# Gated linear attention and an MLP on one core: x of chunks 2 to 5 turned by DMA instead of TensorE

## The chip, the core and the metric

The kernel runs on one NeuronCore of a Trainium2 chip. Its engines work side by side, each through its own instructions in the order of the program: TensorE (PE) multiplies matrices and writes to PSUM; VectorE (DVE), ScalarE (ACT) and GpSimd (POOL) work element by element; SyncE (SP) only issues DMAs. They wait for each other by semaphores. The metric is the device time of one execution in microseconds (us), lower is better.

## The reference

Per batch (4) and head (8), a state of 48 x 48 runs over 768 tokens; its output, the eight heads side by side, is the input x of a block with layer norm, two matrix products and a residual:

```
state = alpha[t][:, None] * state + outer(k[t], v[t]);  y[t] = q[t] @ state
x  = y of all heads, 384 columns
xn = (x - mean(x)) / sqrt(var(x) + 1e-6) * g_ln
out = x + maximum(xn @ w_ch1, 0) @ w_ch2          # 384 -> 1536 -> 384
```

Everything is float32.

## The kernel before, in words

The 768 tokens are cut into six chunks of 128. One chunk of one batch, 128 tokens of all eight heads, is called a block here; there are 24. `attention(c, b)` is the work of a block, written as a generator: each `yield` ends a turn. In its first turn it takes the logarithm of alpha (`la`, L293), then come the running sums (L525, in `sums`), exponentials (L303, L304), the products with q and k (L312), the turning of q and k on TensorE (L349, copied from PSUM by L359), the scores (L541, masked by L383), the updates of the state (L399, L412, L414) and y (L440). ACT copies y to SBUF as `x` (L452 or L456), SP keeps a copy in DRAM (`kept`, L466), and ACT normalizes it to `xn` (L473 to L483).

The MLP wants x with columns on partitions, as `xT`. For chunks 2 to 5 (`c >= IN_HALVES`, 16 blocks) a float32 is seen as two 16-bit halves, and TensorE turns each half exactly, as bfloat16, in pieces of 64 x 64: 24 transposes a block (L506) into two PSUM banks. In the next turn ACT copies each bank to `xT`, putting the halves of a number together again (L510). Chunks 0 and 1 are turned in float32 (L490).

From chunk 1 on, the MLP's two products are made from 15 and 20 block products instead of the 18 and 24 that plain multiplication by blocks takes. So `combine_x` (L830) adds and subtracts blocks of `xT` on DVE, `hidden_product` (L856) multiplies, DVE and POOL add up (L866 to L899), ACT takes the Relu (L907), `combine_hidden` (L663) adds blocks of that, and `product` (L676) multiplies again and adds to the output (L686 to L755), which `send` (L555) stores. `outputs` (L551) loads the kept x again as `ob` for that.

The order of all this is written by hand. `ORDER` is a string of 1501 letters; each letter gives one generator one more turn: `a` to `x` are the 24 blocks, `M`, `V`, `N`, `X` and `R` the MLP, `O` the outputs, `0` to `3` the loads. Every engine gets its instructions in that order, and so does SP's one queue of DMAs.

Tiles with the same tag share buffers: `la`, `x` and `xn` share the tag "row" with eight buffers of 1.5 KB a partition, and all PSUM tiles share eight banks. A new tile takes the buffer that has been free longest, and its first writer waits until the last reader of the tile before has ended; if none is free by the program, the instruction waits for the first that becomes so.

Of the kernel before, what the change touches and what calls it, by code (L numbers as in the profile page):

```python
# [9 lines left out]
FP32 = mybir.dt.float32  # L10
# [3 lines left out]
BF16 = mybir.dt.bfloat16  # L14
UINT16 = mybir.dt.uint16
# [4 lines left out]
IN_HALVES = 2  # L20
# [31 lines left out]
def kernel(  # L52
# [36 lines left out]
    nc = tc.nc  # L89
# [4 lines left out]
    P = 128  # L94
# [3 lines left out]
    NF = DM // P  # L98
# [7 lines left out]
    work = ctx.enter_context(tc.tile_pool(name="work", bufs=2))  # L106
    dram = ctx.enter_context(
        tc.tile_pool(name="dram", bufs=B, space=bass.MemoryType.DRAM))
    ps = ctx.enter_context(tc.tile_pool(name="ps", bufs=2, space=bass.MemoryType.PSUM))
# [3 lines left out]
    HS = P // 2  # L113
    halves = [slice(HS * s, HS * s + HS) for s in range(2)]
# [60 lines left out]
    ident_of_halves = consts[:, 2 * P + HS:].bitcast(BF16)  # L175
# [96 lines left out]
    def qk_of(c, b):  # L272
        return qks[b if c == 0 else b ^ 1 if c == 1 else (b ^ 1) % 3]
# [6 lines left out]
    x_of, xT_of, hT_of, las, lps_of, qkT_of, aps_of, ob_of = ({} for _ in range(8))  # L280
# [3 lines left out]
    def attention(c, b):  # L284
# [26 lines left out]
        for n in (0, 1) if whole else (1, 0):  # L311
            nc.vector.tensor_mul(qk[:, n], raws.pop(("qk"[n], c, b)), (eq, lv)[n])  # L312
            if n == 0:
                row = dram.tile([2, 2 * 64 * NP], FP32, name="row", tag="row")
# [9 lines left out]
        if c < IN_HALVES:  # L324
            for i in range(2):
# [5 lines left out]
                tv = tps.rearrange("r p (s t) -> r p s t", s=2)  # L331
# [6 lines left out]
        else:  # L338
            words = qk_of(c, b).rearrange("t n p i c -> t (n p i c)").bitcast(BF16).rearrange(
                "t (n p i c w) -> t n p i c w", n=2, p=NP, i=2, w=2)  # L340
            tps = [ps.tile([P, 512], FP32, name=f"tps{h}", tag="bank", bufs=8) for h in range(2)]
            for n in range(2):
                for p in range(NP):
                    for w in range(2):
                        for i, cs in enumerate((slice(0, 64), slice(64, R))):
                            for h in range(2):
                                tv = tps[h].bitcast(BF16).rearrange(
                                    "r (n p w t) -> r n p w t", n=2, p=NP, w=2)
# [33 lines left out]
        else:  # L382
            nc.vector.copy_predicated(  # L383
                out=at.rearrange("k p s t -> k (p s) t"),
# [36 lines left out]
        for p in range(NP):  # L421
# [4 lines left out]
            for n in range(0 if whole else 8):  # L426

                if odd:
                    inner, s, i = n // 4, n // 2 % 2, n % 2
                    r = i  # L430
                else:
                    i, s, r = n // 4, n // 2 % 2, n % 2
# [17 lines left out]
        if odd:  # L450
            for r in range(2):
                act(out=x[:, r * DM // 2:][:, :DM // 2], func=AFT.Copy, accum_out=few[:, 4 + r:5 + r],  # L452
                    in_=yps[r][:, r].rearrange("t b d -> t (b d)"))
# [14 lines left out]
        xn = work.tile([P, DM], FP32, name="xn", tag="row", bufs=8)  # L468
# [9 lines left out]
        if whole:  # L478
            nc.vector.tensor_scalar(out=xn, in0=x, scalar1=mean, scalar2=rstd,
                                    op0=AOP.add, op1=AOP.mult)  # L480
        else:
            nc.scalar.mul(off, mean, rstd)
            act(out=xn, in_=x, func=AFT.Identity, scale=rstd, bias=off)  # L483
        yield
        if c not in xT_of:
            xT_of[c] = work.tile([P, NF, B, P], FP32, name="xT", tag="xT")
        if c < IN_HALVES:
            xps = ps.tile([P, NF, P], FP32, name="xps", tag="bank", bufs=8)
            for f in range(NF):
                nc.tensor.transpose(xps[:, f], xn[:, f * P:(f + 1) * P], ident)  # L490
            yield
            if whole:
                nc.vector.tensor_mul(xT_of[c][:, :, b], xps,
                                     g_col.unsqueeze(2).broadcast_to([P, NF, P]))
            else:
                nc.vector.tensor_copy(out=xT_of[c][:, :, b], in_=xps)
        else:
            words = xn.bitcast(BF16).rearrange("t (f i c w) -> t f i c w", f=NF, i=2, w=2)
            xps = [ps.tile([P, 512], FP32, name=f"xps{h}", tag="bank", bufs=8) for h in range(2)]
            for f in range(NF):  # L500
                for w in range(2):
                    for i in range(2):
                        for h in range(2):
                            tv = xps[h].bitcast(BF16)[:, :2 * NF * HS].rearrange(
                                "r (f w t) -> r f w t", f=NF, w=2)
                            nc.tensor.transpose(tv[halves[i], f, w], words[halves[h], f, i, :, w],  # L506
                                                ident_of_halves[halves[h]])
            yield
            for h in range(2):
                nc.scalar.copy(  # L510
                    out=xT_of[c][:, :, b, halves[h]].bitcast(UINT16).rearrange(
                        "r f (t w) -> r f t w", w=2),
                    in_=xps[h].bitcast(UINT16)[:, :2 * NF * HS].rearrange(
                        "r (f w t) -> r f t w", f=NF, w=2))
        yield


# [415 lines left out]
    turns |= {"PQ"[h]: second_of_chunk_0(h) for h in range(2)}  # L933
    turns |= {"4": sums(), "5": scores()}
    turns |= {chr(ord("a") + n): attention(n // B, n % B) for n in range(NCB * B)}
    turns |= {chr(ord("A") + i): take_weights(i) for i in range(len(pieces))}
    turns |= {"M": mlp(), "V": hidden_products(NCB - 1), "S": combine_first(), "W": combine_weights(), "R": relus(),
# [34 lines left out]
```

## Time and profile before

| | |
|---|---|
| three runs | 423.15, 423.38, 423.86 us; median 423.38 |
| profiled execution | 423.5 us, the span from its first to its last instruction |
| TensorE clock granted | 1.000 in the whole span |
| L506, turning x on PE | 384 instructions, one 186 to 217 ns, several at a time |
| L510, copying it from PSUM on ACT | 32 instructions, 491 ns each |
| L483, xn of the 20 blocks of chunks 1 to 5 on ACT | 707 ns each |
| DMAs issued by SP | 235, nearly 44 MB in all |

A busy time is the time in which an engine has at least one instruction under way; those of PE overlap, so a share near 100% says that PE is seldom without work, not that it is at its peak. The chain that ended last follows back, from the last instruction, what each step waited for. In lists by group, the numbers behind the bar are the busy time and the mean of one instruction in ns, then the idle time of the engine before them and who ended it.

### The profile page before, as it was taken

What the parts mean: (1) busy time and instruction counts of PE and PEld (TensorE: products, weight loads), DVE (VectorE), ACT (ScalarE), POOL (GpSimd) and SP (SyncE); (2) the same over time, 40 slices, a digit from 0 to 9 for tenths busy, and PEclk for the clock granted to TensorE, in tenths of its full rate; (3) what the DMA queues carried; (4) which work ended last, traced back from release to release, by engine and by line L of the source; (5) the groups of instructions that cost most, each with busy time, mean ns of one, the idle gap of its engine ahead of it and who ended that gap; (6) DMA issues with size and microseconds to landing.
All of it is one profiled execution on the core that took longest, in us unless ns stands there. A gap on an engine that the chain in (4) does not pass through costs nothing.

```text
span 423.5 us, 14142 instructions
## 1 busy us (share of the span) xinstructions
PE 416.0 (98%) x5988; PEld 366.6 (87%) x5988; DVE 326.9 (77%) x626; ACT 228.0 (54%) x572; POOL 155.2 (37%) x182
## 2 busy tenths in 40 slices
PE   7989999999999999999999999999999999999996
PEld 5878878756778889998889998899998899988996
DVE  3689989898998989778668667749676588756684
ACT  6987577969535879434666066496432541124300
POOL 4242010200116391244671334670145650656414
PEclk9999999999999999999999999999999999999999
DMA  7879866774533341161503136002122000130001
GB/s 234 242 210 276 259 180 187 229 224 146 115 109 122 97 147 45 38 180 30 150 23 111 61 90 159 0 22 39 42 82 70 0 2 0 39 112 2 0 20 56
DMA packets 50791, 43.95 MB, mean 104 GB/s; under 512 B 23164, under 2 KB 46844, under 8 KB 50728
## 3 DMA queue, kind: packets, MB, share of 16 engines
q1 hardware_dynamic: 50696, 43.04, 35.3%
q8 instruction: 47, 0.77, 0.8%
q14 instruction: 16, 0.13, 0.1%
q0 software_dynamic: 32, 0.00, 0.0%
HBM read 34.29 MB, written 8.74 MB: 102 GB/s over the span
## 4 chain that ended last, share of the span: by engine, by line
PE 91%; DVE 3%; DMA 3%; ACT 1%; issue 1%; SPq 1%; DVEq 0%
PE ops L676 31%; PE hps L856 31%; PE ops L576 7%; PE hps L564 7%; PE yps L440 5%; PE aps L541 2%; PE ups L399 2%; PE tps L349 2%; DMA ws<-in_moe_w_ch_dram 2%; PE lps L525 1%; DMA ra<-in_alpha_dram 1%; DVE qk L312 1%; PE xps L506 1%; PE tps L328 1%; PE xps L490 1%
## 5 line engine op out<-in xcount | busy, mean ns | idle before, releaser
L692 POOL TENSOR_TENSOR ob<-ob,u 128x192 f32<-128x192 f32 x40 | 25.5, 648 | 88.5 <-DVE ob L689 66.1
L856 PE MATMUL hps<-sum,w 128*128 128x256 f32 x192 | 47.5, 382 | 0.1
L414 POOL TENSOR_TENSOR mid<-mid,gate 112x192 f32<-112x192 f32 x20 | 10.7, 536 | 92.3 <-DVE mid L412 55.2
L856 PEld LDWEIGHTS hps<-sum,w 128*128 128x128 f32 x192 | 36.1, 190 | 5.1 <-DVE qk L312 0.2
L676 PE MATMUL ops<-w,hT 128*128 128x192 f32 x224 | 39.9, 327 | 0.0
L676 PEld LDWEIGHTS ops<-w,hT 128*128 128x128 f32 x224 | 37.0, 190 | 0.3
L564 PE MATMUL hps<-xT,w 128*128 128x256 f32 x144 | 33.6, 385 | 1.1 <-DVE w L233 0.8
L856 PE MATMUL hps<-xT,w 128*128 128x256 f32 x136 | 34.4, 380 | 0.0
L564 PEld LDWEIGHTS hps<-xT,w 128*128 128x128 f32 x144 | 26.5, 190 | 6.6 <-issue 1.1
L576 PE MATMUL ops<-w,hT 128*128 128x384 f32 x96 | 32.0, 488 | 0.0
L907 ACT ACTIVATE hT<-hT 128x512 f32<-128x512 f32 x48 | 27.3, 629 | 7.8 <-POOL hT L894 2.7
L856 PEld LDWEIGHTS hps<-xT,w 128*128 128x128 f32 x136 | 25.8, 190 | 3.5
L676 PE MATMUL ops<-ws,sum 128*128 128x192 f32 x160 | 28.6, 327 | 0.0
L576 PEld LDWEIGHTS ops<-w,hT 128*128 128x128 f32 x96 | 17.9, 190 | 11.5
L686 DVE TENSOR_TENSOR ob<-ops,ob 128x192 f32<-128x192 f32 x50 | 17.0, 351 | 13.0 <-PE ops L676 7.6
L676 PEld LDWEIGHTS ops<-ws,sum 128*128 128x128 f32 x160 | 26.4, 190 | 0.0
L359 ACT COPY qT<-tps 112x512 uint16<-112x512 uint16 x32 | 17.2, 600 | 16.0 <-PE tps L349 16.0
L676 PE MATMUL ops<-ws,hT 128*128 128x192 f32 x128 | 23.4, 326 | 0.0
L510 ACT COPY xT<-xps 128x384 uint16<-128x384 uint16 x32 | 13.5, 491 | 16.9 <-PE xps L506 16.9
L676 PE MATMUL ops<-more,sum 128*128 128x192 f32 x120 | 22.2, 328 | 0.0
L676 PEld LDWEIGHTS ops<-ws,hT 128*128 128x128 f32 x128 | 21.3, 190 | 0.1
L440 PE MATMUL yps<-mid,qT 48*64 48x48 f32 x320 | 20.9, 220 | 0.0
(254 smaller groups left out, 1138.0 us busy)
## 6 DMA issues: line engine op xcount, KB each, us to landing
ws<-in_moe_w_ch_dram SPq DMA_DIRECT2D x12, 768.0 KB, 5.9
vn<-in_v_dram SPq DMA_DIRECT2D x12, 384.0 KB, 3.9
kept<-x SPq DMA_DIRECT2D x20, 192.0 KB, 2.7
ob<-kept SPq DMA_DIRECT2D x20, 192.0 KB, 2.2
out_dram<-ob SPq DMA_DIRECT2D x19, 192.0 KB, 1.9
rq<-in_q_dram SPq DMA_DIRECT2D x16, 192.0 KB, 4.1
rk<-in_k_dram SPq DMA_DIRECT2D x16, 192.0 KB, 4.3
ra<-in_alpha_dram SPq DMA_DIRECT2D x14, 192.0 KB, 2.5
```

What stands on the lines that cost most here:

```text
L349: nc.tensor.transpose(tv[cs, n, p, w], words[halves[h], n, p, i, :cs.stop - cs.start, w], ident_of_halves[halves[h]])
L359: nc.scalar.copy(out=to, in_=tps[h].bitcast(UINT16).rearrange("r (n p w t) -> r n p t w", n=2, p=NP, w=2)[:R, n])
L414: nc.gpsimd.tensor_mul(new, new, by)
L440: nc.tensor.matmul(yps[r][halves[s], i, p], of, by, start=not (odd and inner), stop=bool(inner or not odd), skip_group_check=bool(odd))
L510: nc.scalar.copy(out=xT_of[c][:, :, b, halves[h]].bitcast(UINT16).rearrange("r f (t w) -> r f t w", w=2), in_=xps[h].bitcast(UINT16)[:, :2 ...
L564: nc.tensor.matmul(hps, w1[:, j // 2, f, j % 2 * P:][:, :P], xT_of[0][:, f, bs], start=(f == 0), stop=(f == NF - 1))
L576: nc.tensor.matmul(ops_of[b], hT_of[c][:, j, b], w2[:, j], start=(j == 0), stop=(j == NJ - 1))
L676: nc.tensor.matmul(acc, lhs[:, j], rhs[:, j], start=(j == 0), stop=(j == NT - 1))
L686: nc.vector.tensor_add(x, acc, x)
L692: getattr(nc.gpsimd, f"tensor_{op}")(x, x, y)
L856: nc.tensor.matmul(acc[:, i], w, b, start=True, stop=True)
L907: nc.scalar.activation(out=x, in_=x, func=AFT.Relu)
```

## The change

Only blocks of chunks 2 to 5 change. In the turn in which ACT makes `xn`, POOL parts it into two planes: the lower halves of all 384 numbers of a token, then the upper halves (`planes`). In the turn in which TensorE turned x, SP issues a DMA from SBUF to SBUF that transposes the six squares of 128 x 128 halves (`turned`). In the turn after it, ACT copies the two planes to `xT`, each number's halves side by side, by two copies of 384 elements each, as before. `planes` and `turned` take buffers of the tag "row", which still has eight. Two PSUM banks a block are no longer asked for. `ORDER` is the same.

```diff
             act(out=xn, in_=x, func=AFT.Identity, scale=rstd, bias=off)
+            if c >= IN_HALVES:
+                planes = work.tile([P, 2, NF, P], UINT16, name="planes", tag="row", bufs=8)
+                nc.gpsimd.tensor_copy(out=planes.rearrange("t w f c -> t w (f c)"),
+                                      in_=xn.bitcast(UINT16).rearrange("t (d w) -> t w d", w=2))
         yield
...
-            words = xn.bitcast(BF16).rearrange("t (f i c w) -> t f i c w", f=NF, i=2, w=2)
-            xps = [ps.tile([P, 512], FP32, name=f"xps{h}", tag="bank", bufs=8) for h in range(2)]
-            for f in range(NF):
-                for w in range(2):
-                    for i in range(2):
-                        for h in range(2):
-                            tv = xps[h].bitcast(BF16)[:, :2 * NF * HS].rearrange(
-                                "r (f w t) -> r f w t", f=NF, w=2)
-                            nc.tensor.transpose(tv[halves[i], f, w], words[halves[h], f, i, :, w],
-                                                ident_of_halves[halves[h]])
-            yield
-            for h in range(2):
+            turned = work.tile([P, 2, NF, P], UINT16, name="turned", tag="row", bufs=8)
+            nc.sync.dma_start_transpose(turned.rearrange("r w f t -> r (w f) t"),
+                                        planes.rearrange("t w f c -> t (w f c)"))
+            yield
+            for w in range(2):
                 nc.scalar.copy(
-                    out=xT_of[c][:, :, b, halves[h]].bitcast(UINT16).rearrange(
-                        "r f (t w) -> r f t w", w=2),
-                    in_=xps[h].bitcast(UINT16)[:, :2 * NF * HS].rearrange(
-                        "r (f w t) -> r f t w", f=NF, w=2))
+                    out=xT_of[c][:, :, b].bitcast(UINT16).rearrange("r f (t w) -> r f t w", w=2)[
+                        :, :, :, w], in_=turned[:, w])
```

## The prediction

> **What bounds the kernel now.** I read the page's busy times first, then the chain of work that ended last.
>
> ```profile
> PE 416.0 (98%) x5988; PEld 366.6 (87%) x5988; DVE 326.9 (77%) x626; ACT 228.0 (54%) x572; POOL 155.2 (37%) x182
> PE 91%; DVE 3%; DMA 3%; ACT 1%; issue 1%; SPq 1%; DVEq 0%
> ```
>
> TensorE is busy for 416.0 of 423.5 us and is 91% of the chain: little hides there, and whatever makes PE wait is paid in full. The same chain in order of time shows what the removed transposes (L506) hold of it:
>
> ```profile
> 140.34 0.27 PE xps L506 x19
> 162.31 0.19 PE xps L506 x24
> 175.68 0.46 PE xps L506 x47
> ...
> 337.07 0.71 PE xps L506 x72
> ```
>
> About 0.2 us for each block of 24. The ten such pieces add to 3.4 us. That is all that the change can give. What it may cost is read on ACT, SP and POOL, from the timeline of each (start, length, engine and line):
>
> ```profile
> 148.56 1.13 ACT L907 ACTIVATE hT<-hT 128x512 f32<-128x512 f32 x2
> 149.91 0.71 ACT L483 ACTIVATE xn<-x,few 128x384 f32<-128x384 f32 x1
> 153.57 0.86 ACT L510 COPY xT<-xps 128x384 uint16<-128x384 uint16 x2 [2.96 <-PE xps L506]
> 155.28 1.66 ACT L907 ACTIVATE hT<-hT 128x512 f32<-128x512 f32 x3
> ...
> 152.16 1.47 POOL L882 TENSOR_TENSOR hT<-hT 128x512 f32<-128x512 f32 x1
> ...
> 338.79 1.27 POOL L882 TENSOR_TENSOR hT<-hT 128x512 f32<-128x512 f32 x1
> ...
> 243.11 0.34 SPq L555 DMA_DIRECT2D out_dram<-ob  x1
> ...
> 180.55 0.76 DVE L830 TENSOR_TENSOR sum<-xT 128x256 f32<-128x256 f32 x2
> 182.70 1.35 DVE L383 COPY_PREDICATED at<-consts,aps 128x512 f32<-128x512 int32 x2
> ...
> 182.90 0.84 PE L525 MATMUL lps<-la,consts 64*64 64x384 f32 x6
> ```
>
> The reader is to see that ACT's copy (L510) stands right behind the transposes, with Relus (L907) that PE needs right behind it. ACT works in order, so a late x holds them all.
>
> **Removed.** 384 transposes on PE, at most 3.4 us, and two PSUM banks per block (worth nothing here: PE's waits are short). **Replaced.** The two copies L510 (491 ns each) become two copies from SBUF of the same 384 elements; L293, which reads SBUF, takes 547 ns for 384, so 0 to 0.1 us a block, inside ACT's 46% idle time; without that cover it would be 1.8 us.
>
> **Added on POOL: 16 copies of 768 halves.** No such copy is in the trace. POOL's one-input L380 takes 664 ns for 512 elements and L177 291 for 128, 0.97 ns an element: 0.9 us for 768. Ends: a memset of 1,024 takes 951 ns, so 0.7; two-input L875 takes 1,289 for 512, so 1.9. I take 0.9, the row with one input. POOL has 63% idle time, but it is in order: where it is late, the copy is late, and the copy waits for ACT's xn with POOL's next work behind it. At block 2 that work is L891, whose result goes to the Relus; these are held longer by ACT's own wait.
>
> **Added on SP: 16 DMAs that transpose**, 192 KB each, at the turn where PE had transposed. None is in the trace. Rows of 192 KB, from issue to landing:
>
> ```profile
> kept<-x SPq DMA_DIRECT2D x20, 192.0 KB, 2.7
> ob<-kept SPq DMA_DIRECT2D x20, 192.0 KB, 2.2
> out_dram<-ob SPq DMA_DIRECT2D x19, 192.0 KB, 1.9
> ...
> gate<-row SPq DMA_DIRECT2D x20, 3.5 KB, 3.9
> ```
>
> The last one, which turns rows into columns, needs 3.9 us for 3.5 KB. The ends are 1.9 and 7.8 (q's loads of 384 KB, the slowest row of that list). I take T = 4.0, since gate is the nearest in kind. SP's issue takes 0.3 to 0.6 us as a rule, 2.67 once (182.83); I take 0.5, and keep 2.67 for the range. The traffic, 3 MB in 250 us beside 44 MB, is free.
>
> **Where it falls.** For each block I take the later of: xn done (L483) and POOL free, plus 0.9; SP's previous DMA issued. I add T and compare with the start of L510. Then I carry the lateness on: an instruction begins when its engine is free and what it waits for has ended, durations as in the trace. Blocks are counted in the order of L506.
>
> - Block 1 (140.2): SP is free at 140.6; landing 144.6; the copy began at 141.3. ACT 3 us late, PE 1.
> - Block 2: xn ended at 150.6, now 153.6. POOL's L882 ended at 153.6, now 156.6; planes 157.6; landing 161.7 against 153.6, so ACT is 8.2 late. The third Relu behind the copy ended at 156.9 and PE's L676 needed it at 157.8, 0.9 of slack: PE 7.4 late.
> - Block 3: xn ended at 161.9, now 170.1; planes 171.1; landing 175.6 against 163.2, ACT 12.4. PE's next wait (L676 at 169.7, on L359's copies ended at 167.3) has 2.4 of slack: PE 10.0.
> - Blocks 4 and 5 (175.5): planes and turned lie in the eight buffers "row", which la, x and xn share. At this turn they are all taken: two planes, the xn of block 6 (written at 166), three x (last read by L483 at 195.5, 206.1 and 228.5) and two la, read by PE's L525, which ends at 183.7. So SP waits for L525, now 193.6. First DMA lands at 197.7; the second takes the buffer that the first's planes leave, so it waits for that landing: 201.8. Then 0.8 for the copies, five L830 (2.0) and L383, behind which PE's L399 (183.6) gets its bank: 205.7. PE 22.1 late. Behind SP's wait stand kept<-x, loads of k and v, ob<-kept and gate's columns: the latter is for POOL's L414, which PE's own stall delays as much.
> - Blocks 7 and 8 (242.6): SP stands behind out_dram<-ob (243.1, itself waiting for POOL). Landing 247.5 and 248.0 against 243.0 and 246.1: ACT 4.5 late, PE 2.9.
> - Blocks 10 and 11 (288.6): SP free at 290.7, landing 294.7 and 295.2 against 291.1: ACT 3.6 late, but PE needs nothing from it soon: 0.
> - Blocks 14 to 16 (337): the last xn ended at 334.8, POOL's L881 and L882 hold it until 340.1; planes 341.0, landing 345.2 against 337.8, ACT 7.4. Relus behind it ended at 341.5, PE's L676 needed them at 342.8: 6.2.
> - Blocks 6, 9, 12 and 13: SP is free over 10 us ahead (214.5, 262.2, 290.7): 0. Were that cover gone, each would be like block 10, 3 to 4 us of ACT.
>
> PE's sum: 7.4 + 2.6 + 12.1 + 2.9 + 6.2 = 31.2. The 3.4 us are not taken off once more: PE reaches the same waits sooner and waits longer. The profiled execution lasted its span, 423.5, and the median is 423.4: 423.4 + 31.2 = 454.6. SP's 2.67 for each issue, with a T of 6, would give +50. With T = 1.9 the same working gives +16, with 2.7 +22, with 7.8 +62; with 1.9 us for a POOL copy 6.5 more.
>
> [...]
>
> **The rivals.**
>
> *As fast as a plain copy:* T = 2.7, the row of the same size, 423.4 + 22 = 445. For it: the bytes are the same. Against: two-byte pieces, and gate's 3.9. Chance 0.20.
>
> *Slow transpose:* SP is held for each one, as for 2.67 us at 182.83, or T is 6 to 7.8: 470 to 486, more beyond. For it: gate needs 3.9 us for 3.5 KB, so there it is pieces and not bytes that take the time, and a turned x has many more of them. Against: SP's issues mostly take 0.3 to 0.6 us. Chance 0.18.
>
> *The row buffers don't bind:* a buffer is free at blocks 4 and 5. Then these cost 7 less: 447 at T = 4.0. Against it: the count above. Chance 0.10.
>
> *Faster:* ACT's wait ends before PE needs what stands behind it, in every block, as in blocks 6, 9, 12 and 13. Then 3.4 us are won: 420.0. The point that decides is block 2: planes and transfer would have to be over by 154.5, within 3.9 us of xn, and POOL alone holds it until 153.6. Chance 0.06; no change 0.02.
>
> **How the numbers follow.** The forecast (T of 3.3 to 6, buffers binding) has 0.44: 454.6. Slower holds 0.92, faster 0.06, within 0.2% (0.85 us, about what a measurement can tell from no change; the three runs lie 0.7 apart) 0.02. The range: from 437, T = 1.9 with some help from free buffers, to 487, T = 7.8. Outside lie faster and no change (0.08), the far part of the slow case (0.08) and a little below 437.
>
> **What the profile after would show.** No L506 on PE; POOL copies near 0.9 us; 16 transposing DMAs; the line "ACT xT waits for" no more PE but the DMA, some 20 to 50 us in total. PE's largest new gap at L399, near 193 to 206, behind DVE's L830; SP waiting there for PE's L525. ACT's wait small for blocks 6, 9, 12 and 13. The prediction is wrong if landings come within 2 us, if the DMA's issue holds SP for several us (all later DMAs would slide, the covered blocks too), or if SP does not wait at blocks 4 and 5.

## The result and the profile after

| | before | after |
|---|---|---|
| median | 423.51 us (423.15 to 423.86, 4 runs) | 459.32 us (457.74 to 460.70, 4 runs) |
| profiled execution | 423.5 us span | 457.74 us, of it 456.0 span |
| TensorE clock granted | 1.000 | 0.980 |

The changed kernel takes 1.0835 times as long, with a 95% interval from 1.0798 to 1.0872: 35.8 us more. The prediction was 454.6 with a range from 437 to 487. Of the four runs the two shorter had a granted clock of 0.980, the two longer of 0.974 and 0.973.

First the busy times and the shares of the chain of work that ended last, from the page of the changed kernel:

```profile
PE 419.4 (92%) x5604; PEld 367.1 (80%) x5604; DVE 330.4 (72%) x626; ACT 231.3 (51%) x572; POOL 168.7 (37%) x198
...
PE 69%; ACT 9%; DMA 7%; DVE 5%; POOL 4%; issue 3%; SPq 2%; POOLq 0%; ACTq 0%; DVEq 0%
```

PE lost 384 instructions and yet was busy 3.4 us longer (part of its work ran at half clock, as is shown below), and its share of the chain fell from 91% to 69%. What took its place is ACT, DMA, DVE and POOL, all of them on the chain because PE waited for them. The costliest groups of the same page show the new operations (busy time, mean ns of one, then the idle time of the engine before them and who ended most of it):

```profile
L507 ACT COPY xT<-turned 128x384 uint16<-128x384 uint16 x32 | 17.4, 620 | 50.6 <-DMA turned<-planes 50.6
...
L486 POOL COPY planes<-xn 128x768 uint16<-128x768 uint16 x16 | 14.7, 916 | 41.1 <-ACT xn L483 40.9
```

ACT stood idle for 50.6 us until a transposing DMA landed. The list of waits, by engine, shows how that reached PE (total, times, longest):

```profile
PE ups L399 <- DVE at L383: 10.5, 1, 10.5
PE ops L671 <- ACT hT L902: 10.1, 2, 5.7
PE ops L671 <- DVE sum L658: 1.8, 2, 1.5
PE tps L349 <- issue: 1.6, 1, 1.6
```

The 10.5 us are one gap, near 192 us of the changed kernel (the Relus of L902 are L907 of before). The chain of work in order of time gives that gap piece by piece (start, length, engine and line):

```profile
191.89 1.23 SPq L503
...
193.22 0.53 SPq L466
...
193.81 0.41 SPq L143
...
194.27 0.45 SPq L160
...
194.82 3.76 DMA turned<-planes
...
198.60 1.10 ACT xT L507 x2
...
199.73 0.77 DVE sum L825 x2
...
201.74 0.65 DVE at L383
...
202.43 1.09 PE ups L399 x22
```

SP issues the DMA of block 4, then three transfers that stand ahead of the DMA of block 5 (kept, k, v), then that DMA, whose landing releases ACT, then DVE, then PE.

The next table compares PE's instructions one by one in the two traces: by how many us PE fell further behind between two moments of the kernel before. In code that none of the kernels here changes, their traces lie between 0.2 us behind and 1.8 us ahead of that of before, so only differences between two columns say something, and steps under 1 us do not.

| PE later by, between (us of before) | 130-162 | 162-174 | 174-198 | 198-254 | 254-290 | 290-350 | sum |
|---|---|---|---|---|---|---|---|
| blocks there | 1, 2 | 3 | 4, 5 | 6, 7, 8 | 9, 10, 11 | 12 to 16 | |
| predicted | 7.4 | 2.6 | 12.1 | 2.9 | 0 | 6.2 | 31.2 |
| changed kernel | 6.4 | 2.7 | 12.0 | 3.9 | 1.1 | 6.9 | 33.0 |

The places are the predicted ones, and nearly the sizes, but for one: the 1.1 us of blocks 9 to 11 lie in a pause of PE of 1.6 us at 301 us of the changed kernel, for which the list of waits names no work of these blocks (see the end). The experiments ask whether the reasons are, too.

### The profile page after: what moved, and what is told of

Read it like the earlier page. It is cut to its first block, busy times and chain, and to the rows that moved or that the text cites. A ratio compares the mean times of both kernels' runs of the same rounds, so it can differ in the third digit from the quotient of the medians.

```text
span 456.0 us, 13430 instructions
## 1 busy us (share of the span) xinstructions
PE 419.4 (92%) x5604; PEld 367.1 (80%) x5604; DVE 330.4 (72%) x626; ACT 231.3 (51%) x572; POOL 168.7 (37%) x198
## 4 chain that ended last, share of the span: by engine, by line
PE 69%; ACT 9%; DMA 7%; DVE 5%; POOL 4%; issue 3%; SPq 2%; POOLq 0%; ACTq 0%; DVEq 0%
PE hps L851 22%; PE ops L671 20%; PE ops L571 7%; PE hps L559 6%; DMA turned<-planes 4%; PE yps L440 4%; ACT xT L507 2%; PE aps L536 2%; PE ups L399 2%; ACT hT L902 2%; PE tps L349 1%; PE lps L520 1%; PE tps L328 1%; DVE sum L658 1%; DMA ra<-in_alpha_dram 1%
## 5 line engine op out<-in xcount | busy, mean ns | idle before, releaser
L671 PE MATMUL ops<-w,hT 128*128 128x192 f32 x224 | 42.1, 336 | 11.6 <-ACT hT L902 10.1
L671 PEld LDWEIGHTS ops<-w,hT 128*128 128x128 f32 x224 | 38.0, 195 | 12.9 <-ACT hT L902 10.8
L507 ACT COPY xT<-turned 128x384 uint16<-128x384 uint16 x32 | 17.4, 620 | 50.6 <-DMA turned<-planes 50.6
L681 DVE TENSOR_TENSOR ob<-ops,ob 128x192 f32<-128x192 f32 x50 | 17.1, 352 | 23.7 <-PE ops L671 9.8
L671 PE MATMUL ops<-ws,sum 128*128 128x192 f32 x160 | 29.0, 328 | 2.7 <-DVE sum L658 1.8
L902 ACT ACTIVATE hT<-hT 128x512 f32<-128x512 f32 x48 | 27.2, 622 | 6.7 <-DVE hT L883 2.4
L486 POOL COPY planes<-xn 128x768 uint16<-128x768 uint16 x16 | 14.7, 916 | 41.1 <-ACT xn L483 40.9
L671 PEld LDWEIGHTS ops<-ws,sum 128*128 128x128 f32 x160 | 26.2, 190 | 3.6 <-DVE sum L658 1.8
L571 PEld LDWEIGHTS ops<-w,hT 128*128 128x128 f32 x96 | 17.9, 190 | 11.5
L671 PE MATMUL ops<-ws,hT 128*128 128x192 f32 x128 | 25.1, 342 | 0.5 <-DVE ob L684 0.5
L399 PE MATMUL ups<-vn,qk 64*64 64x48 f32 (+3 forms) x592 | 15.1, 218 | 10.5 <-DVE at L383 10.5
L399 PEld LDWEIGHTS ups<-vn,qk 64*48 64x48 f32 (+3 forms) x592 | 13.5, 131 | 13.2 <-DVE at L383 10.6
```

The lines of the kernel that those rows point to most:

```text
L399: nc.tensor.matmul(up[h, p], qk_of(c, b)[ts, 1, p, i, :h.stop - h.start], vn[ts, i, p], start=True, stop=True)
L486: nc.gpsimd.tensor_copy(out=planes.rearrange("t w f c -> t w (f c)"), in_=xn.bitcast(UINT16).rearrange("t (d w) -> t w d", w=2))
L507: nc.scalar.copy(out=xT_of[c][:, :, b].bitcast(UINT16).rearrange("r f (t w) -> r f t w", w=2)[:, :, :, w], in_=turned[:, w])
L571: nc.tensor.matmul(ops_of[b], hT_of[c][:, j, b], w2[:, j], start=(j == 0), stop=(j == NJ - 1))
L671: nc.tensor.matmul(acc, lhs[:, j], rhs[:, j], start=(j == 0), stop=(j == NT - 1))
L681: nc.vector.tensor_add(x, acc, x)
```

## The experiments

Diffs are against the changed kernel where nothing else is said.

### Nine row buffers

```diff
-        la = work.tile([P, 2, NP, D], FP32, name="la", tag="row", bufs=8)
+        la = work.tile([P, 2, NP, D], FP32, name="la", tag="row", bufs=9)
```

and the same for the four other tiles of the tag.

> The tag row gets nine buffers in place of eight; nothing else is changed. If SP's wait for a row buffer at blocks 4 and 5 (4.6 us of waiting for PE's running sums) is a cause, the first of the two DMAs goes out as soon as SP is free, near 187 in place of 191.9, and PE's gap before L399 shrinks from 10.5 us to 4 to 6: 451 to 455 us. Rival: the DMAs' own time on SP and in the queue decides, and the buffer is only the last of several waits that end together: 458 to 460.

Measured: 456.28 us (453.49 to 457.61), ratio 1.076 [1.0719, 1.0801]: between the two. SP's queue in the timeline of this kernel (start, length, line, tile, count):

```profile
187.35 1.31 SPq L503 DMA_TRANSPOSE turned<-planes  x1
188.75 0.53 SPq L466 DMA_DIRECT2D kept<-x  x1
189.33 0.42 SPq L143 DMA_DIRECT2D rk<-in_k_dram  x1
189.85 0.40 SPq L160 DMA_DIRECT2D vn<-in_v_dram  x1
190.35 1.21 SPq L503 DMA_TRANSPOSE turned<-planes  x1
```

The wait for a buffer is gone, and the DMA of block 4 leaves 4.5 us earlier than in the changed kernel. But the DMA of block 5 lands 6.1 us after its issue instead of 3.8, and PE fell 10.9 us behind in this stretch instead of 12.0. The queue ahead of that DMA isn't the difference: the same three transfers (kept, k and v) stand the same 1.6 us ahead of it in both kernels. In this profile its own packets slowed down, from 0.02 us each to 0.18 us on average between 193.0 and 193.5, beside a load of instructions:

```profile
q8 instruction: 1, 0.02, 1.0%
```

This is the line of the "instruction" queue (packets, MB, share) in the list of DMAs between 190.35 and 196.5; in the changed kernel no such packet moved during this DMA. So the buffers did hold SP. Between the medians they are worth 3 us; the profile, with this one slow landing in it, shows 1.1 us at this place (for such landings see the end).

### No parting on POOL

```diff
-            act(out=xn, in_=x, func=AFT.Identity, scale=rstd, bias=off)
-            if c >= IN_HALVES:
-                planes = work.tile([P, 2, NF, P], UINT16, name="planes", tag="row", bufs=8)
-                nc.gpsimd.tensor_copy(...)
+            if c < IN_HALVES:
+                act(out=xn, in_=x, func=AFT.Identity, scale=rstd, bias=off)
+            else:
+                act(out=xn, in_=x, func=AFT.Identity, scale=0.0)
...
-                                        planes.rearrange("t w f c -> t (w f c)"))
+                                        xn.bitcast(UINT16))
```

> POOL's 16 copies are left out: the DMA turns xn's bytes as they lie. So that these bytes stay finite, xn of chunks 2 to 5 is written as zero (Identity with scale 0, the same length on ACT), and the MLP of these chunks works on zeros. If POOL's place in its order holds blocks 2 and 16 (5 and 8 us of lateness there, of which POOL's two earlier additions make 3 and 5), the gaps of PE before L671 near 158 and 368 nearly vanish and the one near 193 stays: 445 to 450 us. Rival: only the DMA's time counts; POOL's copy is in series at a few blocks, 0.83 us each: 456 to 458.

Measured: 449.3 us (447.76 to 452.6), ratio 1.0614 [1.0565, 1.0663], inside the expectation. By stretch, PE fell behind by 7.3, -0.3, 12.2, 2.7, 1.7 and -0.2 us. With scale 0 ACT's xn took 0.51 us and not the 0.71 of the changed kernel, so up to 0.2 us a block is its part. But for that, at block 3 and at the end the whole loss hung on POOL, whose sums (L876 and L877, L881 and L882 of before) stood ahead of the parting. At block 2 POOL was not alone: SP's queue in this kernel shows who was second.

```profile
150.30 3.95 SPq L143 DMA_DIRECT2D rq<-in_q_dram  x2
154.35 1.24 SPq L502 DMA_TRANSPOSE turned<-xn  x1
```

The issue of two loads of q ended at 154.25, so the DMA left only 1.2 us earlier than in the changed kernel (155.58). It then landed 4.45 us after its issue instead of 2.90, and PE was no earlier: taking POOL away bought nothing there in this profile. In both kernels the loads of q stood ahead of it and a load of instructions ran beside it, so why the landing took 1.5 us more stays open.

### Each DMA twice

```diff
             nc.sync.dma_start_transpose(turned..., planes...)
+            nc.sync.dma_start_transpose(turned..., planes...)
```

> Each transposing DMA is issued twice, into the same buffer, the second after the first has landed: T goes from 2.8 to about 5.7. If ACT's wait for the landing is what costs, six landings stand in series on the way to PE and some more count in part, 7 to 8 us for each us of T: 22 us more, 478 to 486. Rival: the places are held by POOL's order and the row buffers, and the transfer lies beside that: under 465.

Measured: 492.08 us (491.14 to 494.1), ratio 1.162 [1.1583, 1.1656], 32.8 us above the changed kernel and more than expected. The time from a DMA's issue to x is on the path, at almost 12 us for each us (32.8 us for the 2.8 us that one landing takes in this kernel), what follows from it included. By stretch the loss grew by 6.4, 2.7, 6.8, 6.7, 0.9 and 10.5 us: everywhere but at blocks 9 to 11. A term that the expectation didn't have is in the next line of the page, the granted clock in tenths, in 40 slices of the span:

```profile
PEclk9999999999998799859999986999799997999999
```

The clock was halved for 51 us in all, in the changed kernel for 17. PE worked for some 27 us of these stretches, there for some 10. In the changed kernel PE worked on 8 of L671's products in the 2.50 us from 203.5 at half clock and on 25 in the 3.70 us from 206.2 at full clock, about half the rate. If half of PE's time in such stretches is lost, an estimate from these two windows that is used below too, 8.5 us more were lost there; without them the time would lie inside the expectation.

### The DMA one turn earlier

```diff
                 nc.gpsimd.tensor_copy(out=planes..., in_=xn...)
+                turned = work.tile([P, 2, NF, P], UINT16, name="turned", tag="row", bufs=8)
+                nc.sync.dma_start_transpose(turned..., planes...)
         yield
...
-            turned = ...
-            nc.sync.dma_start_transpose(...)
             yield
```

> The DMA is issued one turn earlier, right behind POOL's copy, in the turn in which xn is made; turned then takes the buffer when planes has just got one. In blocks 4 and 5 the landing is over long before ACT's copy and no buffer is missing: the gap near 193 vanishes. Blocks 2, 3 and 16 have xn, parting and DMA in series as before and stay late. 444 to 449 us. Rival: SP, which now waits for POOL earlier in its order, holds the loads behind it, and what is won is lost again: 455 or more.

Measured: 445.94 us (445.6 to 446.3), ratio 1.0524 [1.0502, 1.0546], as expected. By stretch: 6.0, 2.8, -0.3, 4.9, 1.2, 7.4. The loss at blocks 4 and 5 is gone: there the DMA lacked only an earlier issue. At blocks 1 to 3 and at the end nothing changed, because xn and POOL are late there, not the issue. And a loss of 4.9 us came up near block 6, where there had been none. SP's lines there, from the timeline:

```profile
199.26 1.05 SPq L316 DMA_DIRECT2D row<-eq  x2
212.10 1.25 SPq L489 DMA_TRANSPOSE turned<-planes  x1
```

ACT's line, with its idle time and what ended it:

```profile
216.16 0.49 ACT L456 ACTIVATE x<-yps 128x384 f32<-128x384 f32 x1 [4.14 <-issue]
```

SP issued nothing from 200 to 212, since it waited for block 6's planes, for which POOL's sums came first. That DMA landed 3.98 us after its issue, at 216.1, and in the same moment ACT could write the next x, which PE's L399 then waited for. That x asked for the row buffer which the DMA had just left fits to 0.1 us; that it was this buffer is not shown, no run had more of them.

### The parting alone, and the DMA alone

Against the kernel before, with all of its transposes kept and nothing reading the new results:

```diff
+            if c >= IN_HALVES:
+                planes = work.tile([P, 2, NF, P], UINT16, name="planes", tag="row", bufs=8)
+                nc.gpsimd.tensor_copy(...)
```

> The kernel before, with POOL's 16 copies added and nobody reading them; TensorE turns x as before. If POOL's time matters only through ACT's wait, this costs what POOL's Relu inputs are late by, under 2 us: 423.5 to 425.5. Rival: POOL's load as such (13 us, some of it ahead of the sums that the Relus wait for) is a large part of the loss: 430 or more.

```diff
+            turned = work.tile([P, 2, NF, P], UINT16, name="turned", tag="row", bufs=8)
+            nc.sync.dma_start_transpose(turned..., xn.bitcast(UINT16))
```

> The kernel before, with the 16 transposing DMAs added on SP at the turns of the changed kernel, reading xn itself and writing a row buffer that nobody reads; TensorE turns x as before, no parting. ACT waits for no landing. The theory of ACT's wait expects little, only SP's wait for a row buffer at block 4, which delays the loads and gate columns behind it: 423.5 to 429. Rival: SP's 20 us of issuing and the queue's traffic delay the loads and stores: 435 or more.

Measured: 424.38 us (423.91 to 425.0), ratio 1.0015 [0.9998, 1.0032], for the 16 copies on POOL; 427.44 us (426.86 to 428.34), ratio 1.0088 [1.0059, 1.0117], for the 16 DMAs. Both as expected. The second loses its time in one place, between 174 and 198 us, where PE fell 2.4 us behind: SP waited 5.6 us for PE's L399 to free a row buffer, and loads stood behind it. So 15 us of POOL's work and the traffic of 16 transposing DMAs are worth under 5 us together where nobody waits for their results; the rest of the 35.8 comes with that waiting.

### The copies to xT on POOL instead of ACT

```diff
-                nc.scalar.copy(
+                nc.gpsimd.tensor_copy(
```

> The two copies from turned to xT go to POOL; ACT waits for no landing, POOL does. The theory of ACT's wait: the Relus and evictions behind the copy are on time at blocks 1 to 3 and 14 to 16, while POOL's own sums are late in their place; the gap near 193, which waits for xT itself, stays: 449 to 455. Rival: it doesn't matter who copies, x itself is needed at once everywhere: 458 or more.

Measured: 456.77 us (454.36 to 458.65), ratio 1.077 [1.0732, 1.0807], between the two. By stretch: 1.0, 3.2, 14.3, 3.1, 1.2, 6.9. At blocks 1 and 2 ACT's wait was the cause: with ACT free, its Relus came in time, and 5.4 us were saved. At blocks 4 and 5 the loss grew by 2.3 us instead. There DVE needs x itself at once, POOL's four copies took 738 ns each instead of ACT's 620, which is 0.5 us, the second DMA landed after 4.45 us instead of 3.76, and the half clock behind the gap, 13.7 us long instead of 10.2, cost 0.7 us more. At the end the loss stayed. One place was about the queue behind the wait, the other about the awaited thing.

### Only chunk 4 by DMA

```diff
-            if c >= IN_HALVES:
+            if c == 4:
```

with the transposes on TensorE for chunks 2, 3 and 5.

> Only chunk 4 is turned by DMA (blocks 9 to 12); the other twelve blocks go through TensorE as before. There SP is ahead of ACT's copy by 10 us in two of four blocks and ACT has slack in the others; 0.8 us of transposes leave PE's chain: 422.5 to 424.0. Rival: each DMA costs wherever it stands: 426 or more.

Measured: 425.13 us (424.07 to 426.88, 12 runs), ratio 1.0036 [1.002, 1.0052]. The expectation was missed: not even this chunk is free. The chain of work of this kernel shows where, at blocks 10 and 11:

```profile
288.21 0.55 SPq L389
...
288.81 0.55 SPq L564
...
289.46 3.02 DMA turned<-planes
...
292.50 2.18 ACT xT L507 x4
...
296.26 2.84 PE ops L689 x16
```

The DMA of block 10 stands behind the gate's columns (L389) and the load of a kept x (L564), and the copies of two blocks behind its landing. PE fell 1.8 us behind between 292 and 303.

### Only the four covered blocks by DMA

```diff
-            if c >= IN_HALVES:
+            if (c, b) in ((3, 0), (4, 1), (4, 2), (5, 1)):
```

> By DMA only the four blocks that the prediction put at no lateness (blocks 6, 9, 12 and 13 in order: chunk 3 batch 0, chunk 4 batches 1 and 2, chunk 5 batch 1); the other twelve are turned on TensorE as before. Theory (a turning hurts only where what it makes is needed at once; elsewhere work ahead of the wait covers it): 422.5 to 424.0 us, no slower than before, at most 0.9 us faster, since 4 of 16 blocks give up at most a quarter of the 3.4 us. Rival (every DMA and every POOL copy costs something, a sixteenth of the 35.8 us each): 431 to 434 us.

Measured: 422.7 us (421.84 to 424.57, 12 runs) against 423.92 (17 runs), ratio 0.998 [0.9965, 0.9995]. As expected: in these four blocks ACT waited for no DMA at all, and PE was on time to the end. The gain of 0.2% is at the limit of what can be told; that they cost nothing is clear. This is the only form of the change that was not slower.

### Only blocks 4 and 5 by DMA

```diff
-            if c >= IN_HALVES:
+            if (c, b) in ((2, 3), (2, 2)):
```

> By DMA only blocks 4 and 5 in order (chunk 2, batches 3 and 2), the others on TensorE. Theory (the place itself costs the time: two turnings one behind the other, and DVE and PE behind them): PE late by 10 to 13 us between 186 and 210 us of before, half clock there again, and 433 to 438 us in all. Rival (the place costs only because PE came to it late already, and because the row buffers were held by the blocks before it): under 430 us.

Measured: 443.21 us (441.6 to 444.5), ratio 1.0448 [1.0413, 1.0483], more than either expected. PE fell 12.8 us behind between 174 and 198, as much as with all sixteen, and 1.7 us just before. So the place has its price of its own, whatever went before it. Of the 5.7 us that came later, where no block is turned by DMA, 3.2 us are two pauses of PE (see the end), and 1.7 us come from another 3.4 us at half clock, from 294.8, right behind the second pause.

### Filling PE's longest gap

```diff
+        for _ in range(22 if (c, b) == (4, 0) else 0):
+            nc.tensor.matmul(ups[0].rearrange("r p d -> r (p d)"), ident[:, :R], w2[:, 0, :NP * D],
+                             start=True, stop=True)
         for p in range(NP):
             for s, up in enumerate(ups):
```

> The changed kernel with 22 products on PE ahead of the updates of block (chunk 4, batch 0), between 192 and 202 us, into the bank that the updates then overwrite; nothing reads them. They keep PE busy for some 9 us in its longest gap. Theory (the clock falls because PE has stood still, and that costs another 1.8 us after the gap: 3.7 us at half clock): full clock from 192 to 206 us, and 456.5 to 458.5 us, against 459.3 without them. Rival (the clock falls for another reason, the number of DMAs or the load of the other engines): half clock there as before, and 459 to 461 us.

Measured: 461.37 us (459.3 to 461.88), ratio 1.0881 [1.0855, 1.0907]: no gain. In the windows of both kernels the columns are the stretch, its length, busy times with counts of PE, PE's loads, DVE, ACT and POOL, then the granted clock, DMA share and GB/s. The changed kernel:

```profile
161.70:165.10 3.40, 2.94 (x9) 2.94 (x10) 0.36 (x1) 3.27 (x14) 0.16 (x1) 0.51 0.03 8
195.90:202.40 6.50, 0.00 (x0) 0.00 (x0) 2.60 (x7) 3.77 (x12) 0.00 (x0) 0.50 0.86 208
202.40:206.10 3.70, 3.67 (x36) 3.58 (x37) 2.55 (x6) 0.78 (x3) 0.00 (x0) 0.50 0.00 0
373.40:376.80 3.40, 3.13 (x10) 3.13 (x11) 2.24 (x4) 1.89 (x4) 0.00 (x0) 0.50 0.02 5
```

With the fill:

```profile
192.10:203.90 11.80, 8.36 (x79) 7.92 (x77) 3.36 (x9) 5.59 (x16) 0.00 (x0) 1.00 0.72 167
203.90:207.30 3.40, 3.40 (x11) 3.40 (x12) 2.06 (x6) 0.06 (x1) 0.14 (x1) 0.50 0.02 5
```

The products took 7.40 us, full clock lasted to 203.9, and the DMAs and the other engines were nearly as busy as without it. So it is PE's standing still that halves the clock here, and the rival falls. But 3.4 us of gap were left, and that was enough to halve the clock again, now for 3.4 us in which PE worked: about the 1.8 us that the fill was to save. Above that, the half clock came elsewhere: near 160 and 375 us it lasted 6.8 us, where it lasts 3.4 in the changed kernel, and 3.4 us more began at 279.0. In all PE worked for some 17 us at half clock, without the fill for some 10, so 3.5 us more were lost. And PE's pause (see the end) took 2.4 us, at 222.6, instead of 1.6. So the time of the whole kernel doesn't say what the gap's half clock costs; the windows do.

### Eight blocks, four of them early

```diff
+EARLY = ((2, 3), (2, 2), (3, 3), (3, 2))
+BY_DMA = EARLY + ((3, 0), (4, 1), (4, 2), (5, 1))
```

> The four blocks of the last but third experiment (6, 9, 12 and 13 by DMA, issued in the turn of the old transposes) and four more by DMA (4, 5, 7 and 8 in order), whose DMA is issued one turn earlier, behind the parting, where the earlier issue of all sixteen let PE be no later between 178 and 202 us and between 214 and 274 us of before; the other eight on TensorE. Theory (a turning whose result is asked for long after its issue costs nothing, and PE gains some 0.2 us for each block): 421.5 to 423.5 us, a ratio of 0.994 to 0.999. Rival (without the lateness that blocks 1 to 3 gave to PE, the DMAs of blocks 4 and 5 come too late even one turn earlier): 425 us or more, with half clock near 190 us.

Measured: 429.35 us (428.76 to 431.7), ratio 1.0144 [1.012, 1.0167]: the rival's time, but not by its mechanism: in the profiled execution the granted clock was 1.000, and ACT did not wait for blocks 4 and 5. From the timeline of this kernel, POOL's line, with its idle time and who ended it:

```profile
163.62 4.89 POOL L488 COPY planes<-xn 128x768 uint16<-128x768 uint16 x1 [2.68 <-ACT xn L485]
```

ACT's:

```profile
168.54 0.52 ACT L295 ACTIVATE la<-ra 128x384 f32<-128x384 f32 x1 [3.85 <-POOL planes L488]
```

And SP's:

```profile
168.54 1.34 SPq L492 DMA_TRANSPOSE turned<-planes  x1
```

POOL's copy, 0.83 us in the median of the changed kernel, took 4.89. By the profile ACT's next logarithm waited 3.85 us for it, which reads like a wait for the row buffer of the xn that the copy was still reading; SP had waited 13.2 us for it. PE fell 4.7 us behind there, and 2.6 us between 198 and 254, where 1.8 us are again a pause of PE (see the end). So at block 4 the early DMA moved the wait from ACT's queue to SP's and POOL's, and to the buffers; what DVE did beside POOL's slow copy is taken up at the end.

## Why the prediction was right, and where its steps were not

**That the removed transposes are worth little: right.** PE is no less busy than before (419.4 us, 416.0 before), and even the four blocks that cost nothing gave 0.2%.

**T = 4.0: mis-sized.** Of the 162 transposing DMAs in all the traces, 59 had no other DMA issued in the 2 us before them and no load of instructions beside them; these landed 2.7 to 2.9 us after the start of their issue. Right behind kept, k and v (the second DMA of blocks 4 and 5) it took 3.8 to 4.5 us, and 6.1 in the kernel with nine buffers. At the seven landings of the changed kernel that hold up PE (blocks 1 to 5, 7 and 16) it was 2.7 to 4.5, on average 3.3. The list of one tile's instructions has the issue (shortest, median, longest ns):

```profile
L503 SPq DMA_TRANSPOSE turned<-planes x16: 1210/1240/2904, 139.9 to 366.8; - x16
```

So SP is held for 1.24 us, not 0.5. The first rival's T, the 2.7 of kept, holds for an undisturbed landing, 2.7 to 2.9 us; the issue is 0.6 us or more above the 0.3 to 0.6 that a plain one mostly takes. (The prediction's "2.67 once" for a plain issue was itself short: in the trace of before six of the 235 issues take over 2 us, the longest 3.67.) By the prediction's own working the rival's T of 2.7 gave +22; measured were +35.8. What made up the difference, each item from the trace:

- half clock: PE was busy for 9.7 us of the windows shown at half clock, which is about 4.9 us lost by the estimate above. The prediction had no such term;
- ACT's copies, 620 ns instead of 491 from PSUM: 0.26 us a block;
- the longer issue, and the transfers ahead of the DMA on the queue: at blocks 4 and 5 SP's chain from 191.89 to the second DMA's start was 2.9 us;
- a pause of PE of 1.6 us at 301. The prediction had no such term either.

So the sum was right to 4.7 us partly by luck: a T too long by 1.2 us, or by 0.7 at the landings that count, stood in for terms that were missing.

**Blocks 1 and 2 (7.4; measured 6.4): right in size, incomplete in cause.** ACT's wait with the Relus behind it is shown by the copies on POOL, which took it away. That POOL alone held block 2 is not: without the parting, SP's loads of q held the DMA nearly as long, and its landing was slower.

**Block 3 (2.6; 2.7) and blocks 14 to 16 (6.2; 6.9): right.** Without the parting both are gone.

**Blocks 4 and 5 (12.1; 12.0): right in size, half wrong in cause.** The row buffers held SP, as forecast. But the second DMA did not wait for the first one's landing; it found a buffer, and stood behind three transfers on SP. The rival by which buffers that don't bind save 7 us was wrong in its price: nine buffers saved 3 us between the medians. In the profile they saved 1.1, with the second landing 2.4 us slower than in the changed kernel.

**Blocks 7 and 8 (2.9; 3.9 with block 6): right within what the table can tell.** Issued early they cost nothing visible in the comparison.

**Blocks 10 and 11 (0): right here, but not as a rule.** In the changed kernel PE falls no further behind between 292 and 303 (0.1 us); the 1.1 us of the table's column 254-290 are the pause at 301. With chunk 4 alone the two blocks cost 1.8 us, so where PE is on time, ACT's lateness does reach it there, through DVE's sums.

**Blocks 6, 9, 12 and 13 (0): right.** The kernel with these alone is no slower.

Of the rivals, a plain copy's T was the true one, without its time; the slow transpose held SP as it said, but for 1.24 us as a rule and not 2.67 (one issue took 2.90); faster was only to be had by choosing four blocks.

## What to carry to other kernels

Where a bound engine does small work for others, moving that work to a DMA trades its time (0.2 us a block here) for a latency (2.7 to 2.9 us for an undisturbed landing here, up to 6.1), and the latency is paid wherever the result, or anything queued behind its reader, is needed before it. Work out that slack block by block, on every in-order queue and every shared buffer that the new steps touch; move only the blocks that have it, and count an idle TensorE again for the clock it loses (here 0.50 for 3.4 to 10.2 us, beside gaps of 4.3, 5.7 and 10.5 us).

## What was not expected of the hardware

**Half clock after a gap.** In the changed kernel PE stood still from 191.9 to 202.4 us; the granted clock was 0.50 from 195.9 to 206.1, so it fell 4.0 us after PE stopped and came back 3.7 us after PE resumed. With the fill, a gap of 3.4 us sufficed, and the half clock came only when PE worked again. The stretches are 3.4 us long or a multiple of it, up to 10.2 us in the changed kernel, 13.7 with the copies on POOL and 17.1 with each DMA twice. Each of the three gaps of the changed kernel that a half clock followed cost 1.5 to 1.8 us beyond itself, by the estimate above. Nor did PE have to stand still for a whole stretch of 3.4 us: with the fill the half clock from 279.0 followed 3.4 us in which PE was busy for 1.97 us, and with blocks 4 and 5 alone the one from 294.8 followed 3.4 us with 1.66 us of work. How much idle time it takes stays open.

**POOL's copy beside DVE's additions.** In two kernels the first parting, with no other POOL work near, took 4.88 and 4.89 us while DVE ran operations with two inputs in SBUF, most of them additions, one behind the other, each in 0.55 to 0.96 us; with the parting alone, two such copies took 1.29 and 0.97 us, and two of DVE's additions beside them 1.04 and 1.30 us instead of 0.68. That DVE's additions slow POOL's copy, and not something else, is not shown: no run took them away.

**Pauses of PE beside loads of instructions.** In the nine kernels in which PE came more than 5 us late, it paused once or twice, for 1.5 to 2.4 us, in the middle of the 128 small transposes of q and k (L349), with nothing in the lists of waits that it waited for; never in the kernel before. The chain of work of the changed kernel, at the only such place:

```profile
300.19 0.94 PE tps L349 x103
301.13 1.61 issue
302.74 0.36 PE tps L349 x19
```

What the list of waits lacks, the list of DMAs has, here between 300.2 and 302.8:

```profile
q8 instruction: 1, 0.02, 2.3%
```

The profile calls this queue "instruction". It moved 47 packets of 16 KB in the kernel before and 44 in the changed one, one for about 255 instructions of PE with its weight loads. In all ten pauses such a packet moved, and PE went on 1.2 to 1.5 us after the packet's end. In the kernel before and in the changed one, from 90 us on, the other runs of 128 take 1.0 to 1.2 us from the start of the first transpose to that of the last. From 90 us on no run of 128 without a pause had such a packet start in its first 0.9 us. That PE waits there for its own next instructions is a guess of the author's; no run shows it.

**Slow landings beside the same loads.** Of the transposing DMAs with no other DMA issued in the 2 us before them, the 59 beside which no instructions were loaded landed after 2.7 to 2.9 us, the 20 beside which one of these packets moved after 2.9 to 4.6, median 4.2. Of all 162, the 18 that held SP for more than 1.5 us, up to 2.9, had such a packet beside them. In the changed kernel it was so at block 3, which landed after 3.4 us, and at block 7, after 4.5. That the load slows the DMA, and not something else both, is not shown.
